# A new issue order, new engines for the evacuations and new PSUM places in a one-core kernel of a long convolution and a token-mixing MLP

## The chip, the core and the metric

The kernel runs on one core of a Trainium2 chip. A core has five engines with a queue of instructions each: PE (TensorE, matmuls; PEld are its weight loads), DVE (VectorE), ACT (ScalarE), POOL (GpSimd) and SP (SyncE, which here only issues transfers). Each queue runs in order, and queues wait for one another by semaphores. Transfers issued from SP, from POOL and, once, from ACT are carried out by DMA engines, 16 for the core. The metric is the device time of one execution in microseconds: the median of three runs before the change is 170.21 (170.05 to 170.65). A profile shows one execution, with times counted from its first instruction.

## The reference, cut to what matters

```python
def _A_ref(q, k, v, shift_k, ssm_k, ssm_D):      # S = 2048 positions, D = 448 channels
    k_shift = sum of 4 shifted copies of k, each times a column of shift_k
    kv = k_shift * v
    y = irfft(rfft(kv, 2S) * rfft(ssm_k, 2S))[:S]          # a causal convolution over S
    y = y.astype(bfloat16) + kv * ssm_D
    return q * y

def _B_ref(x, w1, b1, w2, b2):                   # S = 2048, F = 1792
    h = _layernorm(x, axis=-1)
    u = _gelu(jnp.einsum("bsd,sf->bdf", h, w1) + b1)
    y = jnp.einsum("bdf,fs->bds", u, w2) + b2
    return y transposed to (b, s, d)

x = A_q
h = x + _A_ref(_layernorm(x), A_k, A_v, A_shift_k, A_ssm_k, A_ssm_D)
return h + _B_ref(_layernorm(h), B_w1, B_b1, B_w2, B_b2)
```

## The kernel before

A position s is 16 q + r: partition q (128 of them) and row r (16 rows of 448 channels). The convolution is made of matmuls with tables of sines: two transform stages forward, a product, two stages back. Every operation belongs to a step with a name, a number, and a place in the step: k1.9:8 is the operation 8 of step 9 of the group k1. The groups, in the order of the data:

- **dummy**: matmuls on a constant at the very start. **tables**: the tables of sines (made by VectorE from iotas of POOL, then a Sin on ScalarE: tables.5:3 and tables.6:3 give the two halves of E, tables.7:5 the small table FW and its relations), and the identity ID (tables.3:0). tables.0:5 is a Sin of one element.
- **loads**: on SP. loads.0 to 3 are the four parts of ssm_k (0.5, 0.5, 0.5 and 0.25 MB); loads.4 is shift_k; 5, 6, 8 and 10 are k's row groups 3, 0, 1 and 2; 7, 9, 11 and 12 are v's 0, 1, 2 and 3 (0.46 MB each); 13 and 14 are D and the biases. **xload**: four row groups of x; groups 2 and 3 share memory with two of four shuffle buffers and wait for the last u shuffle.
- **kv**: kv.1 to kv.8 transpose k (two steps for each row group, in the order 3, 0, 1, 2) and copy it out; kv.9 to kv.16 are the shifted product, two steps for each row group: matmuls with the diagonals DG (kv.0:4), then a multiplication by v on VectorE (L1006). **kT**: ssm_k transposed, eight steps.
- **k1, u1** (`emit_stage1`): first transform stage of the kernel ssm_k and of kv. 16 steps each: eight matmuls of 32 columns (L1058), one evacuation of 896 elements (operation 8), and after every second step three shuffles, two on POOL (9, 10) and one on SP (11), at L1074. Four steps share one of four shuffle buffers; a buffer is free when its shuffles have landed.
- **k2, u2** (`emit_stage2`): second stage; four matmuls a step (L1093, 64 columns), evacuations 4 and 5 in the odd step.
- **i1** (`emit_products_i1`): 16 products on VectorE (L1160, step operation 0; the first waits for every shuffle), matmuls (L1177), evacuations, and shuffles into TZ (L1201; L1188 for the last step, i1.16).
- **q, xn**: statistics of the 16 rows of x on VectorE (L1237) and their roots on POOL; xn normalises rows 0 to 3 (L1270 on ScalarE, L1272 on VectorE). **ct, ct0**: transposed tables. **warm**, **ew**, **bias**: small things.
- **i2** (`emit_i2`): the last stage and the layernorm of h, row by row: matmuls (L1303, L1309), a gate (L1319 or L1321), a combine on VectorE (L1329, L1339), squares on ScalarE (L1357), a chain on POOL, and Q[r] on VectorE (L1388). i2.8 makes Q[0], i2.21 combines row 3; i2.58, i2.67 up to i2.97 are matmuls of rows 9 to 15, and rows 14 and 15 (i2.93, i2.97) need the small transfers of TZ's last columns.
- **w1a, w1b, w2**: loads of the MLP's weights on SP: four parts of W1A (0.917 MB, four rows r each; the last three wait for the last TZ shuffles), four of W1B, four of W2.
- **mlp** (`emit_mlp`): mlp.0 to 15: row r times seven column blocks of W1A, in seven PSUM banks (L1435); mlp.17 to 23: the other seven blocks, 16 matmuls each (L1445), Gelu on ScalarE (L1425); mlp.24 to 39: output row r, 14 matmuls (L1457), an evacuation with the residual on VectorE (L1460), output transfers. mlp.39, the last row, is cut in a part of 320 (0 to 13) and one of 128 columns (16 to 29).

Nothing chooses at run time. `ORDER` lists, for each of the five queues, the operations in the order in which they are issued; where an operation may run on two engines (an evacuation, xn, a gate), the list in which it stands decides. `SLOTS` gives every group of matmuls its PSUM bank or pair of banks, and every shuffle or product buffer its place, in the order of use. `schedule` walks these lists with estimated times only to find which operation is the last to be waited for; `emit` writes out instructions and semaphore waits. The rest of the file says what each operation computes.

## Time and profile before

| | us |
|---|---|
| median of three runs | 170.21 |
| span of the profiled execution | 168.7 |
| PE busy | 160.0 |
| DVE busy | 101.7 |
| ACT busy | 90.3 |
| POOL busy | 58.8 |

The profiled execution's own span is 168.7 us from its first instruction to its last; 1.5 us lie around it in the timed median. A view by windows gives, for each stretch, its length, the busy time of PE, PEld, DVE, ACT and POOL with the number of instructions, the granted clock of PE (1.00 is full), the busy share of the DMA engines and GB/s. The chain of waits lists the work that ended last, back to what released it, as start, length and what. A timeline merges instructions of one kind that follow each other; in brackets stands how long the engine was idle before, and who released it. A line of the view of one source line gives the least, median and greatest duration in ns and the first and last start.

### The profile page before, as it was taken

To read this page: it belongs to the slowest core of one execution; us is meant where nothing else is said; L and a number is where in the kernel's file an instruction comes from. 1 tells how busy PE (TensorE), PEld (TensorE's weight loads), DVE (VectorE), ACT (ScalarE), POOL (GpSimd) and SP (SyncE) were. 2 spreads that over 40 slices of the span, in tenths; PEclk is the share of its full clock that TensorE was granted. 3 is DMA by queue.
4 is the path that set the end of the run, shared out by engine and by line. 5 is a ranking of instruction groups with operands and counts; after the bars stand their busy time and mean duration, and the time that the engine had idled before them with its cause. 6 is when DMAs were issued, how large, how long until landed. Compare 5 with 4: busy or idle time off the path is not lost.

```text
span 168.7 us, 3563 instructions
## 1 busy us (share of the span) xinstructions
PE 160.0 (95%) x1416; PEld 92.4 (55%) x1416; DVE 101.7 (60%) x191; ACT 90.3 (54%) x130; POOL 58.8 (35%) x155
## 2 busy tenths in 40 slices
...
## 3 DMA queue, kind: packets, MB, share of 16 engines
q1 hardware_dynamic: 12396, 28.26, 46.1%
...
## 4 chain that ended last, share of the span: by engine, by line
PE 62%; ACT 15%; DVE 10%; DMA 6%; issue 3%; POOL 1%; DVEq 0%; ACTq 0%; POOLq 0%
PE ps L1457 25%; PE ps L1435 13%; PE ps L1445 13%; ACT arena L738 7%; DMA arena<-arena 6%; ACT arena L1068 4%; ACT arena L739 4%; DVE arena L1160 2%; PE ps L1309 2%; PE ps L1058 2%; PE ps L1037 2%; PE ps L1093 2%; DVE arena L741 2%; DVE arena L837 1%; PE ps L1177 1%
## 5 line engine op out<-in xcount | busy, mean ns | idle before, releaser
L1460 DVE SCALAR_TENSOR_TENSOR arena<-ps,arena 128x448 bf16<-128x448 f32 (+2 forms) x17 | 11.1, 656 | 55.8 <-PE ps L1457 55.8
L1457 PE MATMUL ps<-arena 128*128 128x448 bf16 (+2 forms) x238 | 42.7, 342 | 0.0
L1457 PEld LDWEIGHTS ps<-arena 128*128 128x128 bf16 x238 | 33.3, 145 | 9.5
L1435 PE MATMUL ps<-arena 128*128 128x448 bf16 x112 | 23.5, 353 | 0.0
L738 ACT CAST arena<-ps 128x896 bf16<-128x896 f32 (+1 forms) x29 | 23.1, 933 | 0.0
L1068 ACT CAST arena<-ps 128x896 bf16<-128x896 f32 x24 | 20.2, 920 | 4.8 <-PE ps L1058 3.3
L1445 PE MATMUL ps<-arena 128*128 128x448 bf16 x112 | 22.3, 352 | 0.0
L1074 POOL DMA_DIRECT2D arena<-arena x32 | 17.7, 558 | 8.6 <-ACT arena L1068 8.5
L1425 ACT ACTIVATE arena<-ps,arena 128x448 bf16<-128x448 f32 x14 | 8.2, 632 | 19.3 <-PE ps L1445 10.3
L1093 PE MATMUL ps<-arena 128*64 128x448 bf16 x128 | 15.3, 361 | 2.0 <-ACT arena L739 0.9
L1435 PEld LDWEIGHTS ps<-arena 128*128 128x128 bf16 x112 | 10.7, 98 | 10.8 <-DVE arena L1388 1.3
L1445 PEld LDWEIGHTS ps<-arena 128*128 128x128 bf16 x112 | 11.0, 98 | 10.2
L1160 DVE TENSOR_TENSOR arena<-arena 128x1792 bf16<-128x1792 bf16 x16 | 16.5, 1084 | 0.0
L1177 PE MATMUL ps<-arena 64*128 64x448 bf16 x128 | 14.1, 351 | 1.1 <-ACT arena L738 0.5
L1058 PE MATMUL ps<-arena 128*32 128x448 bf16 x256 | 14.6, 355 | 0.5 <-ACT arena L1068 0.2
L1201 POOL DMA_DIRECT2D arena<-arena x16 | 9.3, 586 | 13.8 <-ACT arena L738 12.9
L1093 PEld LDWEIGHTS ps<-arena 128*64 128x64 f16 x128 | 5.3, 108 | 11.2 <-ACT arena L739 3.4
L1177 PEld LDWEIGHTS ps<-arena 64*128 64x128 f16 x128 | 5.2, 94 | 9.8 <-DVE arena L1160 3.1
L1388 DVE TENSOR_SCALAR arena<-arena 128x448 bf16<-128x448 f32 x16 | 7.6, 509 | 4.8 <-POOL arena L1381 4.8
L1058 PEld LDWEIGHTS ps<-arena 128*32 128x32 f16 x256 | 5.1, 95 | 7.8 <-ACT arena L1068 2.6
L1237 DVE BATCH_NORM_STATS2 arena<-arena 128x6 f32<-128x448 bf16 x16 | 9.4, 612 | 0.0
L739 ACT ACTIVATE arena<-ps 128x896 bf16<-128x896 f32 x10 | 8.6, 926 | 0.8 <-PE ps L1093 0.8
...
## 6 DMA issues: line engine op xcount, KB each, us to landing
...
```

Source lines behind the costliest of these rows:

```text
L738: return e.copy(out=dst(), in_=src())
L739: return e.activation(out=dst(), in_=src(), func=ACT.Copy, scale=scale)
L1058: op("pe", lambda e, W, b=b, r=r, q=q, x=x, c0=c0: e.matmul(PS[32 * q:32 * q + 32, b.slots[x], 0:D], E[:, 2 * r + x, c0:c0 + 32], src[:, r ...
L1068: return e.copy(out=dst, in_=Ppair(b)) if W == "act" else e.tensor_copy(out=dst, in_=Ppair(b))
L1074: shuf[tag].append(op(q_, lambda e, W, g=g, i=i, a=a, nu=nu, jh=jh: e.dma_start(T[a + i:a + i + 4 * nu - 3:4].rearrange("p (j k) c d -> p ...
L1093: op("pe", lambda e, W, b=bs[h], h=h, j=j, c=c, par=par: e.matmul(PS[64 * par:64 * par + 64, b.slots[c], 0:D], FW[:, 64 * c:64 * c + 64], ...
L1160: op("dve", lambda e, W, m=m, i=i: e.tensor_tensor(out=MR(m.slots[0]).rearrange("p (x y) d -> p x y d", x=2), in0=TU[:, i].unsqueeze(2).br ...
L1177: k = op("pe", lambda e, W, b=bs[h], m=ms[h], par=par, t=t, tab=tab, xy=xy, P=P: e.matmul(Pb(b, par), tab[P, :], MR(m.slots[0])[P, xy, :], ...
L1435: op("pe", lambda e, W, r=r, fc=fc, b=bs[fc]: e.matmul(Pb(b), W1A[:, r, 128 * fc:128 * fc + 128], Q[:, r, :], start=(r == 0), stop=(r == R ...
L1445: op("pe", lambda e, W, r=r, fc=fc, b=b: e.matmul(Pb(b), W1B[:, r, 128 * (fc - n0):128 * (fc - n0) + 128], Q[:, r, :], start=(r == 0), sto ...
L1457: op("pe", lambda e, W, r=r, fc=fc, b=b, d0=d0, d1=d1: e.matmul(Pb(b)[:, d0:d1], W2[fc // 7][:, fc % 7, r:S:R], G[:, fc, d0:d1], start=(fc ...
L1460: op("dve", lambda e, W, r=r, b=b, A=A, d0=d0, d1=d1: e.scalar_tensor_tensor(out=XR(r)[:, d0:d1], in0=Pb(b)[:, d0:d1], scalar=bm[:, r:r + ...
```

## The change

Both lists are replaced as a whole; no operation is added or taken away, and the functions stay as they are. The new lists come from a search of order, engines and places whose model of the transfers lets all queues share the 16 DMA engines. All lines behind the lists move down by 24.

31 operations change between ScalarE and VectorE. To VectorE go kv.6:12, ct0.0:8, bias.0:1, ten evacuations of 896 elements (u1.1, u1.2, u1.8, u1.11, u1.13, k2.5:5, k2.9:5, k2.15:4, u2.11:4, u2.3:5) and the gate i2.68. To ScalarE go kT.1 to kT.5 (without kT.0), kv.7:8, seven evacuations of 896 elements (k1.12, u1.3, u1.12, u1.15, k2.9:4, i1.10:18, i1.6:9), xn.1 and the gates i2.55, i2.81, i2.85. The diff, cut:

```diff
--- before.py
+++ after.py
     "pe": (
-        "dummy.0:1-9 kv.4:0-11 kv.3:0-7 kv.6:0-11 kv.5:0-7 kT.1:0-7 kT.0:0-3 kT.1:9-11 kT.0:4-7 kT.3:0-7 "
-        "kT.2:0-3 kT.3:9-11 kT.5:0-7 kT.2:4-7 ct0.0:0-7 kT.6:0-7 kT.7:0-7 bias.0:0 kv.7:0-7 k1.8:0-7 k1.9:0-7 "
-        "k1.12:0-7 k1.10:0-7 kv.1:0-7 kv.2:0-11 k1.11:0-7 k1.15:0-7 k1.14:0-7 k1.13:0-7 kT.4:0-7 kv.8:0-11 "
...
-        "i2.54:0-1 i2.28:0-1 i2.32:0-1 warm.1:0 mlp.0:2-6 i2.58:0-1 mlp.0:0-1 mlp.1:0-6 i2.67:0-1 mlp.2:0-6 "
...
-        "mlp.36:0-13 mlp.37:0-13 mlp.38:0-13 mlp.39:0-10 mlp.39:16-17 mlp.39:11 mlp.39:18-20 mlp.39:12 "
-        "mlp.39:21-22 mlp.39:13 mlp.39:23-29 "
+        "dummy.0:1-9 kv.3:0-7 kv.4:0-11 kv.1:0-7 kv.2:0-11 kv.7:0-7 kv.8:0-11 kT.4:0-7 kv.9:0-27 kv.10:0-23 kT.5:0-7 "
+        "kT.1:0-7 kT.1:9-11 u1.0:0-7 u1.1:0-7 kT.6:0-7 kT.7:0-7 u1.2:0-7 u1.3:0-7 kT.3:0-7 kv.5:0-7 kT.3:9-11 "
+        "kT.0:0-7 kT.2:0-7 k1.8:0-7 k1.12:0-7 kv.15:0-27 k1.9:0-7 kv.6:0-11 k1.10:0-7 k1.0:0-7 k1.11:0-7 k1.13:0-7 "
+        "kv.12:0-23 k1.14:0-7 k1.1:0-7 k1.15:0-7 k1.2:0-7 kv.14:0-23 k1.4:0-7 k1.5:0-7 kv.11:0-27 k1.6:0-7 k1.7:0-7 "
+        "k1.3:0-7 u1.4:0-7 kv.13:0-27 u1.5:0-7 u1.6:0-7 kv.16:0-23 u1.7:0-7 u1.8:0-7 u1.9:0-7 u1.10:0-7 u1.11:0-7 "
+        "ct0.0:0-7 u1.12:0-7 u1.13:0-7 u1.14:0-7 u1.15:0-7 k2.12:0-3 k2.13:0-3 k2.0:0-3 k2.1:0-3 k2.6:0-3 k2.7:0-3 "
+        "k2.9:0-3 k2.8:0-3 k2.10:0-3 k2.11:0-3 k2.4:0-3 k2.5:0-3 k2.14:0-3 k2.15:0-3 u2.0:0-3 u2.1:0-3 u2.8:0-3 "
+        "u2.9:0-3 u2.12:0-3 u2.13:0-3 u2.4:0-3 u2.5:0-3 u2.7:0-3 u2.6:0-3 i1.1:10-17 i1.1:1-8 k2.3:0-3 k2.2:0-3 "
...
+        "ct.0:0-7 ct.1:0-7 bias.0:0 i2.1:0-3 i2.9:0-3 ct.2:0-7 i2.10:0-1 i2.2:0-1 warm.0:0 i2.45:0-1 i2.28:0-1 "
+        "i2.17:0-1 i2.54:0-1 i2.41:0-1 warm.1:0 i2.20:0-1 i2.58:0-1 i2.32:0-1 mlp.0:2 mlp.0:1 mlp.0:3 mlp.0:0 "
+        "i2.67:0-1 mlp.1:1 mlp.0:5 mlp.1:3 mlp.1:0 mlp.1:2 mlp.0:6 i2.71:0-1 mlp.0:4 mlp.1:5-6 mlp.2:0 mlp.2:5 "
+        "mlp.2:1-2 mlp.1:4 i2.80:0-1 mlp.2:3 mlp.2:6 mlp.3:1 mlp.3:6 mlp.2:4 mlp.3:5 i2.84:0-1 mlp.3:2 mlp.3:4 "
+        "mlp.3:0 mlp.3:3 mlp.4:4 mlp.4:6 i2.93:0-1 mlp.4:1 mlp.5:6 mlp.5:4 mlp.4:2-3 mlp.4:5 mlp.5:1 mlp.5:5 mlp.4:0 "
+        "mlp.6:6 mlp.6:1 mlp.5:2 i2.97:0-1 mlp.5:0 mlp.6:5 mlp.5:3 mlp.6:3 mlp.7:5 mlp.7:3 mlp.6:0 mlp.7:0 mlp.8:0 "
+        "mlp.6:4 mlp.8:3 mlp.9:0 mlp.10:0 mlp.7:1 mlp.8:1 mlp.9:1 mlp.9:3 mlp.6:2 mlp.19:0 mlp.7:4 mlp.8:5 mlp.10:1 "
+        "mlp.19:1 mlp.10:3 mlp.7:6 mlp.8:4 mlp.7:2 mlp.19:2 mlp.9:4 mlp.10:4 mlp.19:3 mlp.8:2 mlp.11:3-4 mlp.11:1 "
...
+        "mlp.38:9 mlp.35:13 mlp.39:5-6 mlp.38:10 mlp.39:7-9 mlp.36:12-13 mlp.38:11-12 mlp.39:24 mlp.38:13 mlp.39:25 "
+        "mlp.39:10 mlp.39:26-29 mlp.39:11-13 "
     ),
     "act": (
     "act": (
-        "tables.0:5 kv.4:12 kv.3:8 kv.6:12 tables.5:3 tables.6:3 ct0.0:8 bias.0:1 tables.7:5 k1.8:8 k1.9:8 "
-        "k1.10:8 k1.11:8 k1.13:8 k1.14:8 k1.15:8 k1.4:8 u1.0:8 u1.1:8 u1.2:8 u1.4:8 k1.5:8 k1.6:8 k1.7:8 u1.5:8 "
-        "u1.6:8 u1.7:8 u1.8:8 u1.9:8 k2.1:4 k2.13:5 k2.5:4-5 k2.9:5 u1.10:8 u1.13:8 u1.14:8 u1.11:8 k2.3:4 "
-        "k2.7:4 k2.11:4 k2.15:4-5 u2.13:4 u2.1:4 u2.9:4-5 u2.7:4-5 i1.1:9 i1.1:18 u2.11:4 i1.14:9 i1.14:18 "
-        "u2.11:5 i1.8:9 i1.8:18 i1.10:9 u2.5:4-5 u2.3:5 i1.12:9 i1.12:18 u2.3:4 i1.6:18 u2.15:5 u2.15:4 i1.4:17 "
...
+        "tables.5:3 kv.3:8 kv.4:12 kT.4:8 kv.7:8 kT.5:8 kT.1:8 u1.0:8 tables.6:3 kT.3:8 u1.3:8 kT.2:8 k1.12:8 k1.8:8 "
+        "k1.9:8 k1.10:8 k1.11:8 k1.13:8 k1.14:8 k1.15:8 tables.0:5 k1.4:8 k1.5:8 k1.6:8 k1.7:8 u1.4:8 u1.5:8 u1.6:8 "
+        "u1.7:8 u1.9:8 u1.10:8 tables.7:5 u1.12:8 u1.14:8 u1.15:8 k2.13:5 k2.1:4 k2.7:4 k2.9:4 k2.11:4 k2.5:4 "
+        "k2.15:5 u2.1:4 u2.9:4-5 u2.13:4 u2.5:4-5 u2.7:4 i1.1:18 u2.7:5 i1.1:9 k2.3:4 i1.14:18 i1.14:9 i1.10:18 "
+        "u2.11:5 i1.10:9 i1.8:9 i1.8:18 i1.6:18 u2.3:4 i1.6:9 i1.12:18 i1.12:9 u2.15:4-5 i1.4:8 i1.4:17 xn.1:0 "
+        "i1.16:9 i1.16:18 xn.2:0 ct.0:8 xn.5:0 ct.2:8 ct.1:8 xn.4:0 i2.46:0 i2.29:0 i2.55:0 i2.19:0 i2.59:0 i2.22:0 "
...
     ),
     "dve": (
-        "dummy.0:0 tables.3:0-1 kv.0:3 tables.6:0 tables.4:16 tables.5:0 tables.4:17 tables.6:1 tables.4:18 "
-        "tables.5:1 tables.4:19 tables.6:2 tables.4:20 tables.5:2 kT.1:8 tables.7:6 kT.0:8 kT.3:8 tables.7:4 "
-        "tables.7:7 kv.5:8 kT.5:8 kT.2:8 kT.7:8 kT.6:8 bias.1:0 kv.7:8 k1.12:8 kv.1:8 kv.2:12 kv.0:4 kT.4:8 "
-        "kv.8:12 kv.12:25 kv.12:24 kv.9:28 kv.10:24 kv.9:29 kv.10:25 kv.11:28-29 k1.0:8 k1.1:8 u1.3:8 q.1:2 "
-        "kv.13:28-29 q.2:0 kv.14:25 kv.14:24 k1.2:8 k1.3:8 q.2:2 q.1:0 kv.15:29 kv.15:28 k2.1:5 q.2:1 q.2:3 "
-        "k2.13:4 q.4:0 q.1:1 kv.16:25 kv.16:24 k2.9:4 q.1:3 u1.12:8 u1.15:8 q.3:2 k2.3:5 k2.7:5 k2.11:5 q.4:2 "
-        "q.3:3 u2.13:5 q.3:0 u2.1:5 i1.0:0 i1.1:0 i1.13:0 i1.14:0 i1.9:0 i1.7:0 i1.8:0 i1.10:0 i1.12:0 i1.11:0 "
-        "i1.10:18 q.4:3 xn.0:1 i1.5:0 i1.6:0 i1.3:0 i1.6:9 xn.3:1 i1.2:0 i1.16:0 q.4:1 q.3:1 i1.15:0 q.6:0 q.6:2 "
-        "q.5:0 q.5:2 q.6:3 q.5:3 q.5:1 q.8:2 q.6:1 q.8:3 q.7:2 q.8:0 xn.1:0 i2.3:0 i2.11:0 i2.4:0 i2.12:0 i2.5:0 "
-        "i2.13:0 i2.6:0 i2.18:0 i2.21:0 i2.8:0 i2.14:0 i2.55:0 i2.30:0 i2.16:0 q.7:0 i2.34:0 i2.26:0 q.8:1 q.7:1 "
-        "q.7:3 i2.27:0 i2.47:0 i2.43:0 q.8:4 i2.56:0 i2.39:0 i2.40:0 i2.60:0 i2.81:0 i2.69:0 i2.52:0 i2.73:0 "
...
+        "dummy.0:0 tables.5:0-1 tables.3:0 tables.5:2 tables.6:0 kv.0:3 kv.1:8 kv.2:12 kv.0:4 kv.8:12 tables.6:1 "
+        "tables.3:1 kv.9:29 kv.9:28 kv.10:24-25 tables.6:2 u1.1:8 kT.6:8 u1.2:8 kv.5:8 kT.7:8 q.1:2 kT.0:8 q.2:0 "
+        "q.2:2 q.1:3 kv.15:28-29 kv.6:12 q.2:1 k1.0:8 q.4:0 kv.12:25 kv.12:24 q.2:3 k1.1:8 k1.2:8 kv.14:25 "
+        "tables.4:16 kv.14:24 tables.4:17 kv.11:28-29 tables.4:18 q.1:0 tables.4:19 k1.3:8 q.4:1 tables.4:20 q.1:1 "
+        "kv.13:29 tables.7:7 tables.7:6 kv.13:28 kv.16:24-25 u1.8:8 tables.7:4 u1.11:8 ct0.0:8 u1.13:8 q.4:2 k2.13:4 "
+        "k2.1:5 k2.7:5 k2.9:5 k2.11:5 k2.5:5 k2.15:4 u2.1:5 i1.0:0 u2.13:5 i1.1:0 i1.14:0 i1.10:0 i1.9:0 i1.13:0 "
+        "k2.3:5 i1.5:0 i1.7:0 i1.8:0 i1.6:0 u2.11:4 i1.12:0 i1.11:0 u2.3:5 i1.2:0 i1.3:0 q.3:0 xn.0:1 i1.15:0 q.4:3 "
+        "i1.16:0 q.6:0 q.3:1 q.6:2 q.3:2 xn.3:1 q.6:3 q.6:1 q.5:0 q.3:3 q.8:0 q.5:2 q.5:1 q.5:3 q.8:2 q.7:2 q.7:0 "
+        "i2.11:0 i2.3:0 i2.12:0 i2.4:0 bias.0:1 i2.5:0 q.8:1 i2.6:0 i2.18:0 q.7:3 i2.13:0 q.7:1 i2.14:0 i2.8:0 "
+        "i2.21:0 i2.16:0 q.8:3 i2.30:0 i2.68:0 i2.34:0 i2.26:0 q.8:4 i2.43:0 i2.60:0 i2.27:0 i2.47:0 i2.56:0 i2.39:0 "
+        "i2.69:0 i2.40:0 i2.73:0 i2.86:0 i2.52:0 i2.82:0 i2.66:0 i2.53:0 i2.65:0 i2.95:0 i2.78:0 i2.79:0 i2.99:0 "
+        "bias.1:0 i2.92:0 i2.91:0 i2.105:0 i2.104:0 mlp.25:14 mlp.26:14 mlp.29:14 mlp.28:14 mlp.27:14 mlp.24:14 "
+        "mlp.30:14 mlp.33:14 mlp.31:14 mlp.34:14 mlp.32:14 mlp.37:14 mlp.35:14 mlp.36:14 mlp.38:14 mlp.39:30 "
+        "mlp.39:14 "
     ),
     "pool": (
-        "tables.4:0 tables.4:2 tables.4:4 tables.4:6 tables.4:8 tables.4:10 tables.4:12 tables.4:14 tables.4:1 "
-        "tables.4:3 tables.4:5 tables.4:7 tables.4:9 tables.4:11 tables.4:13 tables.4:15 tables.1:0 tables.0:1 "
-        "tables.0:2 tables.0:0 tables.0:3 tables.0:4 loads.13:0 tables.2:0 tables.2:1 tables.2:3 tables.2:5 "
-        "tables.2:7 tables.2:8 tables.2:9 tables.2:10 tables.2:11 tables.2:2 tables.2:4 tables.2:6 q.0:0 q.0:1 "
-        "kv.0:1 kv.0:2 tables.7:0 tables.7:1 tables.7:2 tables.7:3 tables.7:8 tables.7:9 tables.7:10 tables.7:11 "
-        "kv.0:0 k1.9:9 k1.9:10 k1.11:9 k1.11:10 k1.13:9 k1.13:10 k1.15:9 k1.15:10 u1.1:9 u1.1:10 k1.1:9 k1.1:10 "
-        "u1.3:9 u1.3:10 k1.5:9 k1.5:10 u1.5:9 u1.5:10 k1.7:9 k1.7:10 u1.7:9 u1.7:10 u1.9:9 u1.9:10 k1.3:9 "
-        "k1.3:10 q.2:4 q.2:5 q.1:4 xn.3:0 q.1:5 u1.13:9 u1.13:10 u1.11:9 u1.15:9 u1.15:10 u1.11:10 xn.0:0 ew.0:0 "
-        "ew.0:2 ew.0:3 ew.0:1 i1.1:19 i1.1:21 i1.14:19 i1.14:21 i1.8:21 i1.8:19 i1.10:19 i1.10:21 i1.12:19 "
...
+        "tables.1:0 tables.0:2 tables.0:0 tables.0:4 tables.0:3 tables.0:1 tables.2:10 tables.2:7 tables.4:1 "
+        "tables.4:5 tables.2:9 loads.13:0 kv.0:1 tables.2:3 kv.0:2 tables.2:6 q.0:0 tables.2:8 kv.0:0 u1.1:9 u1.3:10 "
+        "u1.3:9 tables.2:5 tables.4:4 tables.4:9 tables.4:8 tables.2:11 k1.9:10 u1.1:10 tables.4:14 tables.4:13 "
+        "tables.4:10 tables.4:7 k1.11:10 k1.9:9 tables.4:15 tables.2:2 tables.4:2 k1.11:9 k1.13:9 tables.4:6 "
+        "tables.4:0 tables.2:0 tables.4:11-12 q.2:4 tables.4:3 k1.13:10 k1.1:9 tables.2:4 k1.1:10 k1.15:10 k1.15:9 "
+        "k1.5:9 tables.2:1 k1.5:10 k1.7:9 tables.7:1 k1.7:10 k1.3:10 tables.7:2 tables.7:0 tables.7:3 k1.3:9 u1.7:10 "
+        "u1.9:10 tables.7:8 u1.9:9 u1.5:10 u1.13:9 tables.7:9 q.0:1 u1.13:10 tables.7:10 u1.5:9 u1.15:9 u1.7:9 "
+        "u1.11:9-10 u1.15:10 tables.7:11 q.2:5 q.1:4-5 ew.0:0 ew.0:2 ew.0:1 i1.1:19 i1.1:21 i1.14:19 i1.14:21 "
+        "i1.10:19 i1.10:21 i1.8:19 i1.8:21 ew.0:3 xn.0:0 i1.6:19 i1.6:21 i1.12:21 i1.12:19 i1.4:20 xn.3:0 i1.4:19 "
...
     ),
     "sp": (
-        "loads.6:0 loads.8:0 loads.0:0 loads.1:0 loads.2:0 loads.3:0 loads.13:1 loads.14:0 loads.14:1 loads.10:0 "
-        "loads.5:0 loads.11:0 loads.4:0 loads.4:1 loads.4:2 loads.12:0 loads.9:0 loads.7:0 k1.9:11 k1.11:11 "
-        "k1.13:11 k1.15:11 xload.0:0 xload.1:0 u1.1:11 k1.1:11 u1.3:11 k1.5:11 u1.5:11 k1.7:11 u1.7:11 u1.9:11 "
-        "k1.3:11 u1.13:11 u1.11:11 u1.15:11 ct0.1:0 ct0.1:1 xload.2:0 xload.3:0 w1a.0:0 ct0.1:2 ct0.1:4 ct0.1:3 "
-        "ct0.1:5 i1.1:20 i1.1:22 i1.14:20 i1.14:22 i1.8:20 i1.8:22 i1.10:20 i1.10:22 i1.12:20 i1.12:22 i1.6:22 "
-        "i1.4:18 i1.16:19 i1.16:20 w1a.1:0 w1a.2:0 w1a.3:0 w1b.0:0 w1b.0:1 w1b.0:2 w1b.0:3 w2.0:0 w2.0:1 w2.0:2 "
-        "w2.0:3 mlp.25:15 mlp.27:15 mlp.29:15 mlp.31:15 mlp.33:15 mlp.35:15 mlp.37:15 mlp.38:15 mlp.39:31 "
+        "loads.6:0 loads.5:0 loads.4:2 loads.10:0 loads.4:1 loads.4:0 loads.2:0 loads.7:0 loads.0:0 loads.3:0 "
+        "loads.1:0 loads.14:0 loads.8:0 xload.0:0 loads.14:1 xload.1:0 loads.12:0 loads.13:1 loads.9:0 loads.11:0 "
+        "u1.1:11 u1.3:11 k1.11:11 k1.9:11 k1.15:11 k1.13:11 k1.7:11 k1.5:11 k1.1:11 k1.3:11 u1.7:11 u1.9:11 u1.5:11 "
+        "u1.13:11 u1.15:11 u1.11:11 ct0.1:1 ct0.1:0 xload.3:0 xload.2:0 w1a.0:0 ct0.1:4 ct0.1:3 ct0.1:5 ct0.1:2 "
+        "i1.14:22 i1.10:22 i1.4:18 i1.16:20 i1.16:19 w1a.1:0 i1.1:20 i1.12:22 i1.14:20 i1.1:22 i1.12:20 i1.8:20 "
+        "i1.6:22 i1.10:20 i1.8:22 w1a.2:0 w1a.3:0 w1b.0:0-3 w2.0:0-3 mlp.29:15 mlp.25:15 mlp.27:15 mlp.33:15 "
+        "mlp.31:15 mlp.35:15 mlp.37:15 mlp.38:15 mlp.39:31 "
     ),
 }
...
```

102 rows, old and new, of tables (ORDER, SLOTS) are left out of this document.

## Prediction

> **What bounds the kernel now.** I read the page first, then the windows, the chain of waits, the timelines of ScalarE and VectorE, and last the landing times of the transfers.
>
> ```profile
> span 168.7 us, 3563 instructions
> PE 160.0 (95%) x1416; PEld 92.4 (55%) x1416; DVE 101.7 (60%) x191; ACT 90.3 (54%) x130; POOL 58.8 (35%) x155
> ```
> ```profile
> 5.00:10.00 5.00, 4.90 (x72) 3.99 (x70) 4.99 (x11) 4.26 (x4) 2.49 (x4) 1.00 1.05 377
> 5.74:70.94 65.20, 61.15 (x876) 30.81 (x874) 62.58 (x95) 59.57 (x71) 35.59 (x67) 1.00 0.80 267
> 2.23:69.01 66.78, 62.99 (x879) 31.57 (x877) 64.16 (x98) 57.89 (x69) 36.64 (x83) 1.00 0.81 274
> 78.26:166.20 87.94, 87.92 (x476) 56.16 (x476) 27.22 (x63) 22.10 (x48) 14.25 (x38) 1.00 0.44 171
> 80.00:84.00 4.00, 4.00 (x23) 2.08 (x23) 4.00 (x16) 2.65 (x7) 3.15 (x7) 1.00 1.06 390
> ```
> ```profile
> 1.52 0.57 POOL arena L779 x2
> ...
> 2.25 1.21 DVE arena L837
> ...
> 4.74 0.60 DVE arena L841
> ...
> 6.09 1.14 DVE arena L844
> ...
> 21.55 6.04 DMA arena<-arena
> ...
> 69.06 0.95 PE ps L1177 x8
> ...
> 70.03 0.91 ACT arena L738
> ...
> 78.26 1.10 PE ps L1435 x5
> ...
> 94.38 1.51 PE ps L1445 x8
> ...
> 123.70 42.08 PE ps L1457 x231
> ...
> 165.81 0.55 DVE arena L1460
> ```
>
> Two machines stand one behind the other. From 78.26 to 166.20 PE is busy 87.92 of 87.94 us at full clock: 476 matmuls, 1.51/8 = 0.19 us for a wide one. No order makes that shorter; it can start earlier or be interrupted. Before it, PE's busy share says little, because there it waits for evacuations: ScalarE is busy 59.57 of the 65.20 us from 5.74 to 70.94, VectorE 64.16 of the 66.78 us from 2.23 to 69.01. The chain passes from the last product to the i1 matmuls (69.06) and the last i1 evacuation (70.03), and i1 ends at 70.94. So the front is bound by ScalarE and VectorE together, with 5.6 and 2.6 us of waiting left in it.
>
> ```profile
> 5.74 2.84 ACT L738 COPY arena<-ps 128x1024 bf16<-128x1024 bf16 x3 [3.23 <-PE ps L965]
> 8.47 3.91 ACT L847 ACTIVATE arena<-arena 128x2048 f16<-128x2048 int32 x2
> ...
> 23.05 0.91 ACT L1068 CAST arena<-ps 128x896 bf16<-128x896 f32 x1 [2.33 <-PE ps L1058]
> ...
> 27.66 5.76 ACT L1068 CAST arena<-ps 128x896 bf16<-128x896 f32 x7 [1.02 <-PE ps L991]
> ...
> 47.98 22.96 ACT L738 CAST arena<-ps 128x896 bf16<-128x896 f32 x28
> ...
> 71.74 2.07 ACT L1270 ACTIVATE arena<-arena 128x448 f32<-128x448 bf16 x3
> ```
> ```profile
> 11.06 1.88 DVE L741 COPY arena<-ps 128x1024 bf16<-128x1024 bf16 x3
> ...
> 20.19 4.38 DVE L1006 TENSOR_TENSOR arena<-ps,arena 128x256 bf16<-128x256 f32 x8
> ...
> 43.58 3.10 DVE L742 TENSOR_SCALAR arena<-ps 128x896 bf16<-128x896 f32 x3
> ...
> 50.05 10.22 DVE L1160 TENSOR_TENSOR arena<-arena 128x1792 bf16<-128x1792 bf16 x10
> ...
> 67.95 1.06 DVE L1160 TENSOR_TENSOR arena<-arena 128x1792 bf16<-128x1792 bf16 x1
> ...
> 68.92 2.19 DVE L1237 BATCH_NORM_STATS2 arena<-arena 128x6 f32<-128x448 bf16 x4
> ...
> 73.95 1.28 DVE L1339 SCALAR_TENSOR_TENSOR arena<-ps,arena 128x448 f32<-128x448 f32 x2 [0.37 <-PE ps L1309]
> ```
>
> The reader sees two prices per evacuation: 896 elements cost ScalarE 22.96/28 = 0.82 us and VectorE 3.10/3 = 1.03; 1024 bf16 elements cost (8.47 - 5.74)/3 = 0.91 from start to start and 1.88/3 = 0.63. He also sees ScalarE's two large holes. At 23.05 it waits 2.33 us, because the last v load lands late and eight kv products then follow in one block on VectorE (4.38 us from 20.19), their matmuls ahead of k1's on PE. At 27.66 it waits 1.02 us, after a shuffle that took 6.04 us to land beside the two x loads.
>
> **The change, part by part.** The arithmetic is the same, so the sum is made of moves. I take the profiled span, 168.7; the median of the runs, 170.21, lies 1.5 above it, and that distance is added back.
>
> (a) Evacuations change engines. ScalarE gives up ten of 896 elements, kv.6 and ct0.0 (12 moves with bias.0, a trifle): 10 x 0.82 + 2 x 0.91 = 10.0 us. It gets seven of 896 elements, five kT, kv.7 and xn.1 (2.07/3 = 0.69): 7 x 0.82 + 6 x 0.91 + 0.69 = 11.9. With bias.0 that is 1.8 us more before i1's end. VectorE gets 10 x 1.03 + 2 x 0.63 = 11.6 and gives 7 x 1.03 + 6 x 0.63 = 11.0, and one bn_stats (2.19/4 = 0.55) moves behind i1: 0.0 to -0.3. So the change adds about 1.5 us of work to a front that both engines bound. It must win it back in waits.
>
> (b) ScalarE begins with tables.5's Sin instead of three copies that wait for k. VectorE now makes tables.5 first, right after POOL's iota (1.52 and 0.57): 1.21 + 0.60 + 1.14, with ID (0.3) between, end near 5.2, where the first copy began at 5.74. Worth -0.5 (bounds -0.8, 0).
>
> (c) Loads. k3 and k2 move to places 2 and 4 of SP's queue, v0 to 8, x0 and x1 ahead of v3, v1, v2. Up to v0 lie 2.36 MB; at the 377 GB/s of 5 to 10 us, begun near 2.5, they are in by 9 to 10 us, and kv.9 and kv.10 run at 10.5 to 12.5. The other six kv pairs are then spread one by one between k1 evacuations, and no x load runs beside the k1 shuffles. So the block at 20.19 and the 6.04 us landing lose their causes: -2.33 and -1.02. New waits: I followed the queues by hand from 19 to 38 us. k1.4 waits for u1.0's buffer (u1.1's shuffle is issued on POOL behind k1.9's, near 22, and lands by the row below at 25.8): 0.6; k1.6 waits for kv.11's matmuls: 0.3; u1.5 for kv.13's: 0.35. That makes 1.25. Bounds: none of it, or all of the 3.35 back.
>
> ScalarE: 70.94 + 1.8 - 0.5 - 3.35 + 1.25 = 70.1, so i1 ends **0.8 earlier**. VectorE as a check: by the same hand count its 2.6 us of waits become 1.2 for k3, k2 and kv.5 in its first 17 us and 0.6 later on, so its last product ends at 69.01 - 0.15 - 2.6 + 1.8 = 68.1, 0.9 earlier. Two engines, one answer; I keep -0.8. Ends: -2.0 with no new wait, +1.3 with all old ones back.
>
> (d) From the last product to the first MLP matmul. VectorE has nine bn_stats behind its last product instead of seven (+1.1), not xn.1 (0.5 less), Q of row 0 now stands ahead of the combine of row 3 (0.6 less), and the wait of 0.37 at 73.95 becomes work: +0.15. i2.58 moves ahead of mlp.0, into time in which PE waits for that Q: 2 x 0.19 = -0.38.
>
> (e) The MLP on PE: same matmuls, chains now shuffled together. W2, at the rate of 390 GB/s behind W1, lands 7 us or more ahead of each first use, though that comes 12 us earlier for its first chunk. What gets tight is SP: after w1a.1 nine small TZ transfers now stand ahead of w1a.2.
>
> ```profile
> L1074 POOL DMA_DIRECT2D arena<-arena x32: 547/547/811, 16.3 to 45.7; - x32
> ...
> DMA to landing us min/median/max: 2.4/3.9/6.0
> ```
> ```profile
> L1201 SPq DMA_DIRECT2D arena<-arena x12: 666/666/683, 54.6 to 69.2; - x12
> ...
> DMA to landing us min/median/max: 3.1/3.7/4.2
> ```
> ```profile
> 75.20 1.47 SPq L1408 DMA_DIRECT2D arena<-in_B_w_dram  x3
> 76.72 7.27 SPq L1412 DMA_DIRECT2D arena<-in_B_w_dram  x4
> ```
>
> Nine issues of 0.666 make 6.0 us. Count from the landing of i1's last transfers (75.20 before, 3.1 us ahead of mlp.0; 3.4 after). w1a.2 is issued 6.5 us later instead of 0.5; three chunks of 0.917 MB at 390 GB/s take 7.05, start and landing 2.3 to 3.0 (estimated from the first w1a issue and the rate), so w1b.0 lands at 16 to 16.6. Its first use, mlp.19:0, is the 73rd matmul after mlp.0 starts: 13.6 + 3.4 = 17.0. Slack 0.4 to 1.0, where before it was several us. i2.93 needs the last small transfer: 0.5 + 8 x 0.666 + 3.1 to 4.2 = 8.9 to 10.0, need 7.2 + 3.4 = 10.6. The rows Q[8] to Q[15] are also wanted 1.5 to 4 us earlier than before, and VectorE's queue there has, by count, under 1 us to spare. I take +0.1; bounds 0 and 2.35, one chunk.
>
> (f) The tail. The last PE work is now the 320-wide part of row 15, and its evacuation comes last. Before, that evacuation (0.55) ran beside seven narrow matmuls, with 0.3 for the narrow one behind it. +0.15, and +0.1 for rows that end bunched and their output transfers: +0.25 (0 to 0.6).
>
> Sum: -0.8 + 0.15 - 0.38 + 0.1 + 0.25 = **-0.7**: span 168.0, median 169.5.
>
> [...] The row says 3.9 in the median. [...]
>
> **The rivals.** (1) *Late u shuffles; slower.* POOL's queue holds u1.7:9, u1.11:9, u1.11:10 and u1.15:10 behind u1.15:9, which waits for the very last u1 evacuation, near 38. At 0.55 each, with the table products between them, the last issue starts near 42.2 by my count, and i1.0, the first product, waits for every shuffle. By the median it lands at 46.1, just behind the time when VectorE comes to i1.0 (45.8, eight k2 and u2 evacuations of 1.03 after 37.6); by the 6.0 of the row at 48.2. Every us behind 46 is a us of i1's end, and the gain is gone from 46.8 on. For: in the profile above the shuffles often took four us and more, and POOL now makes its tables in between. Against: no load runs at that time. At 6.0: +2.1 - 0.3, median 171.3.
>
> (2) *W1 late; slower.* The slack of (e) is missed by a chunk: PE stands at mlp.19:0 or i2.93 for 2.3 us. For: slack under one us. Against: the rate of 390 held steadily. 169.5 + 2.3 - 0.7 of slack: 171.1.
>
> (3) *No change.* The new waits are as long as the old ones less the work added: the model that placed the transfers is no nearer to the chip, and the new order does not do what it says. i1's end moves by 0, the rest by +0.1: 170.3.
>
> (4) *More.* (c) leaves no new wait: -1.25 more, and (b) its full 0.8: 168.0.
>
> **How the numbers follow.** A difference under 0.3%, 0.5 us, cannot be told from none. Forecast 0.42, of which 0.28 lies below 169.7; rival (4) 0.14; (3) 0.10, of which 0.03 slower; (1) 0.17; (2) 0.17. Faster 0.28 + 0.14 = 0.42; same 0.14 + 0.07 = 0.21; slower 0.03 + 0.34 = 0.37. The forecast's own range, from the ends of (b) and (c), is 168.3 to 170.6; with the rivals the range is 167.7 to 171.9.
>
> **What would show it.** (a) ScalarE with 59 instead of 62 evacuations of 896 elements ahead of i1's end, busier by 1.8 us up to there. (b) Sin first on ScalarE, near 5.2. (c) No hole over 1 us on ScalarE between 15 and 38; kv.9's products before 12.5; the shuffle at k1.4 landing by 26. i1's end near 70.1, mlp.0 near 77.2. (e) PE without a gap over 0.3 us at mlp.19:0 and i2.93; nine L1201-type issues on SP behind w1a.1. (f) The last VectorE instruction is the 320-wide one. I am wrong if VectorE or ScalarE stands idle for over 1 us ahead of i1.0 (rival 1), if PE is idle between 84 and 95 (rival 2), or if i1 ends no earlier than 70.9.

## Result: 3.7% slower, and the profile after

| | median, us | lowest to highest | profiled execution's span |
|---|---|---|---|
| before | 170.43 | 170.05 to 171.15 | 168.7 |
| after | 176.94 | 176.02 to 178.24 | 174.2 |

The ratio is 1.0373, with the interval [1.0319, 1.0427]: the new lists make the kernel **slower by 6.5 us** in the median. The forecast was 169.5 with a range of 167.7 to 171.9, so both were wrong. The profiled execution after the change took 176.02, the lowest of the four; its span is 5.5 us longer than that of before, and those 5.5 us are looked for below. The last microsecond of the 6.5 is therefore not placed by the profile. All ratios below are worked out from each kernel's undisturbed executions alone; the profiles of the first kernel of "Repairs together" (175.71 us) and of "old PE rows and banks" (184.03) are of slower ones, and that of the third (174.30) is of the slowest one counted.

The page of the kernel after, first its span and engines:

```profile
span 174.2 us, 3568 instructions
PE 160.5 (92%) x1416; PEld 92.3 (53%) x1416; DVE 100.3 (58%) x188; ACT 93.4 (54%) x133; POOL 61.4 (35%) x155
```

PE's busy time is nearly the same (160.5 against 160.0), with the same 1416 matmuls. The view by windows (start and end, length, busy time of PE, PEld, DVE, ACT and POOL, granted clock, DMA share, GB/s) over ScalarE's and VectorE's stretch up to i1's end, from there to the first MLP matmul, and over two parts of the MLP:

```profile
5.09:72.82 67.73, 61.96 (x896) 32.55 (x893) 63.32 (x100) 61.75 (x73) 35.88 (x86) 1.00 0.79 258
2.23:70.35 68.12, 62.40 (x878) 32.40 (x876) 63.68 (x95) 59.28 (x70) 36.28 (x92) 1.00 0.80 264
72.82:80.88 8.06, 6.37 (x37) 2.97 (x37) 7.61 (x23) 7.43 (x13) 6.03 (x10) 1.00 0.58 178
80.88:101.00 20.12, 18.00 (x91) 8.16 (x90) 14.98 (x45) 14.44 (x35) 16.22 (x37) 1.00 0.88 322
101.00:171.46 70.46, 70.46 (x386) 46.94 (x383) 10.15 (x17) 8.54 (x14) 0.00 (x0) 1.00 0.29 118
```

Four terms come out of these stretches and the rows that bound them. i1 ends at 72.82 instead of 70.94: **+1.88**. From there to the first MLP matmul pass 8.06 us instead of 78.26 - 70.94 = 7.32: **+0.74**. From that matmul to PE's end pass 171.46 - 80.88 = 90.58 instead of 87.94: **+2.64**; PE is busy 18.00 of the first 20.12 us and all of the 70.46 after them, so the loss lies ahead of 101. The tail is 174.2 - 171.46 = 2.74 instead of 168.7 - 166.20 = 2.50: **+0.24**. Together +5.5. The granted clock is 1.00 throughout, so no part of this is a lower clock.

The timeline of ScalarE after, around the new waits of the front (start, length, what; in brackets the idle time before it and who ended it):

```profile
5.09 2.00 ACT L871 ACTIVATE arena<-arena 128x2048 f16<-128x2048 int32 x1 [3.09 <-DVE arena L868]
...
9.60 1.93 ACT L762 COPY arena<-ps 128x1024 bf16<-128x1024 bf16 x2 [0.69 <-PE ps L1061]
11.91 1.01 ACT L762 COPY arena<-ps 128x1024 bf16<-128x1024 bf16 x1 [0.39 <-PE ps L1061]
13.51 1.01 ACT L762 COPY arena<-ps 128x1024 bf16<-128x1024 bf16 x1 [0.59 <-PE ps L1061]
...
28.78 6.81 ACT L1092 CAST arena<-ps 128x896 bf16<-128x896 f32 x8 [1.18 <-PE ps L1082]
...
43.55 1.73 ACT L763 ACTIVATE arena<-ps 128x896 bf16<-128x896 f32 x2 [0.83 <-PE ps L1117]
...
70.81 2.01 ACT L762 CAST arena<-ps 128x896 bf16<-128x896 f32 x2
```

The old holes of the kernel before (2.33 at 23.05, 1.02 at 27.66) are gone. In their place stand many small ones: three at the kT copies (0.69, 0.39, 0.59), 1.18 at k1.4, 0.83 at the second stage. Who made ScalarE wait is read one step further back, on PE:

```profile
8.85 0.71 PE L1061 MATMUL ps<-arena 128*128 128x128 bf16 x8 [0.32 <-DMA arena<-in_A_ssm_k_dram]
...
12.76 0.72 PE L1061 MATMUL ps<-arena 128*128 128x128 bf16 x8 [0.88 <-DMA arena<-in_A_ssm_k_dram]
...
37.13 0.62 PE L1131 MATMUL ps<-arena 128*128 128x128 f16 x8 [0.87 <-DVE arena L1092]
...
42.59 1.71 PE L1117 MATMUL ps<-arena 128*64 128x448 bf16 x16 [0.89 <-DVE arena L766]
...
91.67 0.74 PE L1459 MATMUL ps<-arena 128*128 128x448 bf16 x3 [0.52 <-DVE arena L1412]
...
93.79 1.69 PE L1459 MATMUL ps<-arena 128*128 128x448 bf16 x8 [0.24 <-DVE arena L1412]
...
96.50 1.31 PE L1459 MATMUL ps<-arena 128*128 128x448 bf16 x6 [1.02 <-DVE arena L1412]
```

At 8.85 and 12.76 the transposes of ssm_k wait for its load, 1.20 us together. The line L1412 at 91.67 to 96.50 is VectorE's Q: the MLP's first matmuls wait for rows of the layernorm. VectorE itself had waited, and the timelines of VectorE and POOL say for whom:

```profile
91.10 0.51 DVE L1412 TENSOR_SCALAR arena<-arena 128x448 bf16<-128x448 f32 x1 [0.76 <-POOL arena L1405]
...
95.93 0.93 DVE L1412 TENSOR_SCALAR arena<-arena 128x448 bf16<-128x448 f32 x2 [1.17 <-POOL arena L1405]
```
```profile
29.83 2.17 POOL L1098 DMA_DIRECT2D arena<-arena  x4
...
36.85 1.68 POOL L1098 DMA_DIRECT2D arena<-arena  x3
...
90.35 0.72 POOL L1405 TENSOR_TENSOR arena<-arena 128x2 f32<-128x2 f32 x1
```

How full PE itself was while the front ran, up to 36 us, show the windows of the two kernels, before and then after:

```profile
4.71:36.00 31.29, 30.05 (x564) 19.57 (x565) 29.31 (x51) 25.13 (x29) 17.35 (x33) 1.00 0.95 336
4.71:36.00 31.29, 29.83 (x583) 19.78 (x581) 27.81 (x55) 26.80 (x30) 14.17 (x45) 1.00 0.89 302
```

PE was busy 30.05 of 31.29 us there before, ScalarE only 25.13. L1405 is the last link of POOL's chain for the layernorm, an operation on 128x2 elements, and here it takes 0.72 us. The two rows of L1098 are shuffle issues of the first stage; they come up again where the order of the shuffles is tried.

### The profile page after: what moved, and what is told of

Read it like the earlier page. It is cut to its first block, busy times and chain, and to the rows that moved or that the text cites. A ratio compares the mean times of both kernels' runs of the same rounds, so it can differ in the third digit from the quotient of the medians.

```text
span 174.2 us, 3568 instructions
## 1 busy us (share of the span) xinstructions
PE 160.5 (92%) x1416; PEld 92.3 (53%) x1416; DVE 100.3 (58%) x188; ACT 93.4 (54%) x133; POOL 61.4 (35%) x155
## 4 chain that ended last, share of the span: by engine, by line
PE 59%; DMA 12%; ACT 12%; POOL 7%; issue 3%; SPq 3%; DVE 3%; ACTq 0%; POOLq 0%
PE ps L1481 24%; PE ps L1469 12%; DMA arena<-arena 8%; PE ps L1459 6%; ACT arena L762 6%; PE ps L1201 5%; DMA arena<-in_A_ssm_k_dram 4%; PE ps L1117 4%; ACT arena L1092 3%; PE ps L1082 2%; PE ps L1061 2%; POOL arena L1405 2%; ACT arena L763 2%; DVE arena L1484 1%; POOL arena L1394 1%
## 5 line engine op out<-in xcount | busy, mean ns | idle before, releaser
L1481 PE MATMUL ps<-arena 128*128 128x448 bf16 (+2 forms) x238 | 46.6, 342 | 0.0
L1484 DVE SCALAR_TENSOR_TENSOR arena<-ps,arena 128x448 bf16<-128x448 f32 (+2 forms) x17 | 10.5, 653 | 60.3 <-PE ps L1481 60.1
L1481 PEld LDWEIGHTS ps<-arena 128*128 128x128 bf16 x238 | 32.9, 144 | 11.1 <-DVE arena L1484 0.5
L1469 PE MATMUL ps<-arena 128*128 128x448 bf16 x112 | 27.7, 352 | 0.0
L1459 PE MATMUL ps<-arena 128*128 128x448 bf16 x112 | 25.9, 353 | 1.9 <-DVE arena L1412 1.8
L762 ACT CAST arena<-ps 128x896 bf16<-128x896 f32 x28 | 23.5, 1071 | 0.2 <-PE ps L1117 0.2
L1098 POOL DMA_DIRECT2D arena<-arena x32 | 17.9, 565 | 14.4 <-PE ps L1061 12.2
L1092 ACT CAST arena<-ps 128x896 bf16<-128x896 f32 x23 | 19.4, 918 | 2.4 <-PE ps L1082 1.8
L1459 PEld LDWEIGHTS ps<-arena 128*128 128x128 bf16 x112 | 10.5, 98 | 13.3 <-DVE arena L1412 4.3
L1469 PEld LDWEIGHTS ps<-arena 128*128 128x128 bf16 x112 | 11.0, 98 | 9.2 <-ACT arena L1449 0.2
L762 ACT COPY arena<-ps 128x1024 bf16<-128x1024 bf16 (+1 forms) x11 | 11.3, 1074 | 2.0 <-PE ps L1061 2.0
L1412 DVE TENSOR_SCALAR arena<-arena 128x448 bf16<-128x448 f32 x16 | 7.8, 511 | 5.0 <-POOL arena L1405 4.9
L1381 ACT ACTIVATE arena<-arena 128x448 bf16<-128x448 f32 x14 | 8.0, 571 | 3.8 <-DVE arena L1353 3.7
L1333 PE MATMUL ps<-arena 128*128 128x448 bf16 x32 | 7.8, 353 | 1.9 <-DMA arena<-arena 1.6
```

The source lines that it names most:

```text
L762: return e.copy(out=dst(), in_=src())
L1092: return e.copy(out=dst, in_=Ppair(b)) if W == "act" else e.tensor_copy(out=dst, in_=Ppair(b))
L1098: shuf[tag].append(op(q_, lambda e, W, g=g, i=i, a=a, nu=nu, jh=jh: e.dma_start(T[a + i:a + i + 4 * nu - 3:4].rearrange("p (j k) c d -> p ...
L1459: op("pe", lambda e, W, r=r, fc=fc, b=bs[fc]: e.matmul(Pb(b), W1A[:, r, 128 * fc:128 * fc + 128], Q[:, r, :], start=(r == 0), stop=(r == R ...
L1469: op("pe", lambda e, W, r=r, fc=fc, b=b: e.matmul(Pb(b), W1B[:, r, 128 * (fc - n0):128 * (fc - n0) + 128], Q[:, r, :], start=(r == 0), sto ...
L1481: op("pe", lambda e, W, r=r, fc=fc, b=b, d0=d0, d1=d1: e.matmul(Pb(b)[:, d0:d1], W2[fc // 7][:, fc % 7, r:S:R], G[:, fc, d0:d1], start=(fc ...
```

## The experiments

The theory after this reading: the MLP loses because its matmuls, shuffled across rows, ask for Q sooner than POOL's chain makes it; the front loses because the ssm_k loads land late and because POOL's shuffles are not issued in the order in which they are ready. The rivals: the MLP's loss is that of the weights behind the nine small transfers on SP; and, for the front, that ScalarE and VectorE are bound by their work, so that any wait taken away comes back elsewhere. All kernels start from one of the two kernels' lists and leave every operation as it is, so all compute the same thing. "Front" is all up to the end of i1; "i2 order" is the order from there to the first MLP matmul. Stage times are read from the one profiled execution of each, and "MLP on PE" runs from the first MLP matmul to PE's end. The kernels after, new front alone, old PE rows and banks and rows in order have the same lists up to i1's end, yet their profiles end it at 72.82, 73.32, 73.14 and 72.33: a difference of under a microsecond between two single profiles says little.

| kernel | median, us | ratio to before | i1 end | first MLP matmul | MLP on PE |
|---|---|---|---|---|---|
| before | 170.43 | | 70.94 | 78.26 | 87.94 |
| after | 176.94 | 1.0373 [1.0319, 1.0427] | 72.82 | 80.88 | 90.58 |
| new front alone | 174.06 | 1.0190 [1.0156, 1.0224] | 73.32 | 81.17 | 88.69 |
| new rest alone | 176.69 | 1.0358 [1.0318, 1.0398] | 70.91 | 79.22 | 92.75 |
| one shuffle earlier | 176.81 | 1.0352 [1.0307, 1.0397] | 72.09 | 80.38 | 90.61 |
| ssm_k ahead of v0 | 178.89 | 1.0479 [1.0424, 1.0534] | 74.40 | 82.89 | 90.61 |
| tables early | 178.41 | 1.0442 [1.0402, 1.0481] | 72.82 | 81.14 | 90.58 |
| old PE rows and banks | 182.43 | 1.0664 [1.0609, 1.0719] | 73.14 | 84.12 | 95.63 |
| new front, TZ early | 173.86 | 1.0185 [1.0159, 1.0212] | 73.48 | 81.85 | 88.05 |
| rows in order | 175.72 | 1.0292 [1.0258, 1.0326] | 72.33 | 80.78 | 89.35 |
| shuffles when ready | 175.44 | 1.0274 [1.0253, 1.0295] | 71.52 | 79.90 | 90.59 |
| both repairs | 172.23 | 1.0108 [1.0072, 1.0145] | 71.79 | 79.61 | 88.05 |

### Which half costs what: the new front alone, the new rest alone

The first kernel takes the new lists up to i1 and, on SP, to the end but for the output transfers, with the old order, engines and banks of ct, i2 and the MLP; the second does the opposite.

```diff
 "pe", new front alone
-mlp.0:2 mlp.0:1 mlp.0:3 mlp.0:0 i2.67:0-1 mlp.1:1 mlp.0:5 mlp.1:3
+mlp.0:2-6 i2.58:0-1 mlp.0:0-1 mlp.1:0-6 i2.67:0-1 mlp.2:0-6
...
 "pe", new rest alone
-mlp.0:2-6 i2.58:0-1 mlp.0:0-1 mlp.1:0-6 i2.67:0-1 mlp.2:0-6
+mlp.0:2 mlp.0:1 mlp.0:3 mlp.0:0 i2.67:0-1 mlp.1:1 mlp.0:5 mlp.1:3
```

> The new lists up to i1, SP's list too (without the order of the output transfers), with the order, engines and banks of before for ct, i2 and the MLP. Theory A (the loss is made in separate places: 1.9 us up to i1's end, 0.7 from there to mlp.0, 2.6 in the MLP where rows of Q are asked for before they are made, 0.3 in the tail): only the 1.9 of the front and up to 0.5 behind it remain, 172.3 to 172.8, and PE has no wait for Q over 0.3 us in the MLP. Rival B (the MLP's waits are the late front carried on, whose statistics and Q begin 2 us later): PE still waits 2 us for Q, 174 to 175. Rival C (W1 late, since nine small transfers stand ahead of w1a.2): PE waits over 1 us for a transfer at mlp.19:0 or i2.93, 174.

> The opposite mixture: the lists of before up to i1 with SP's list of before, and the new order, engines and banks for ct, i2 and the MLP. Theory A: 170.4 + 2.6 + 0.3 and up to 0.7 behind i1 = 173.3 to 174.0, and PE waits about 2 us for Q between mlp.4 and mlp.12. Rival B: i1 ends as before and Q is in time, 170.4 to 171.0. Rival C: W1 is issued 6 us earlier here, so nothing is late, 170.4 to 171.0.

With the new front alone the time is 174.06, not the 172.3 to 172.8 that the theory gave but the time that stood for its rivals: i1 ends late (73.32), later than in the kernel after with the same lists, and the MLP is nearly whole (88.69 us). Its PE and window rows:

```profile
98.64 0.93 PE L1439 MATMUL ps<-arena 128*128 128x448 bf16 x4 [0.45 <-DMA arena<-in_B_w_dram]
```
```profile
81.17:101.00 19.83, 19.32 (x101) 9.40 (x101) 14.16 (x40) 13.95 (x34) 13.71 (x37) 1.00 0.86 296
```

In the old order PE does not wait for Q; in the same stretch it does 101 matmuls where the kernel after does 91. The one wait of size is that for W1 at 98.64, 0.45 us: the place that the second rival named, at a fifth of its price.

The second kernel, 176.69 where the theory gave 173.3 to 174.0, is a poor complement. With the old front a root on POOL came late, a gate on ScalarE stood 3.63 us for it, and PE behind the gate. ScalarE, then PE, then the windows of that kernel:

```profile
87.94 0.72 ACT L1337 ACTIVATE arena<-ps,arena 128x448 f32<-128x448 f32 x1 [3.63 <-POOL arena L1266]
```
```profile
88.72 0.93 PE L1327 MATMUL ps<-arena 128*128 128x448 bf16 x2 [3.10 <-ACT arena L1337]
89.44 2.42 PE L1453 MATMUL ps<-arena 128*128 128x448 bf16 x6
92.08 2.43 PE L1453 MATMUL ps<-arena 128*128 128x448 bf16 x12
```
```profile
85.00:90.00 5.00, 1.90 (x8) 0.68 (x6) 3.05 (x10) 1.59 (x4) 3.49 (x8) 0.83 1.05 401
90.00:95.00 5.00, 5.00 (x24) 2.37 (x22) 3.42 (x9) 4.84 (x14) 3.74 (x10) 0.83 1.05 412
```

Its MLP of 92.75 us therefore holds a stall and a slow clock that the kernel after does not have, and the two ratios do not add up to that of the whole change (1.9% and 3.6% against 3.7%). What it does give is the stretch between: with i1's end at 70.91 as before, the first MLP matmul comes at 79.22 instead of 78.26, with the last TZ transfers landing 4.28 us behind i1's end (4.26 before). So the new order of the rest costs up to a microsecond there by itself, as far as one profile of each can say.

### The MLP: rows, banks, weights

"Rows in order" keeps the banks, places and everything else of the kernel after and only sorts the chains of rows 0 to 15 by row, leaving the i2 matmuls and mlp.19 in their places. The chains of mlp.17 and on move behind row 15. "Old PE rows and banks" keeps everything up to mlp.0, and i2 on all engines, in the order after the change; the matmuls of the MLP, the banks from i2.67 on, the MLP's Gelus, evacuations and output transfers take the old order, row by row.

```diff
 "pe", rows in order
-mlp.0:2 mlp.0:1 mlp.0:3 mlp.0:0 i2.67:0-1 mlp.1:1 mlp.0:5 mlp.1:3 mlp.1:0 mlp.1:2 mlp.0:6 i2.71:0-1 mlp.0:4
+mlp.0:2 mlp.0:1 mlp.0:3 mlp.0:0 i2.67:0-1 mlp.0:5 mlp.0:6 mlp.0:4 mlp.1:2 mlp.1:1 mlp.1:3 i2.71:0-1 mlp.1:0
...
```

> The changed kernel with its banks and the places of its i2 matmuls kept, the matmuls of mlp.0 to mlp.15 alone sorted row by row (the chains of mlp.17 and on move behind them, but for mlp.19). By count Q[6] is then asked for 10.3 us after mlp.0, Q[7] at 11.8, Q[10] at 16, and they are made 10.7, 12.9 and 15.5 us after it in the changed kernel. Theory A: one wait of 1.1 to 1.4 us at mlp.7 is left of the 2.9 us of waits, 175.2 to 176.0. If the waits have another cause than the order in which rows are asked for: 2.5 to 3 us of waits stay, 176.6 to 177.2.

> The changed kernel with the MLP's matmuls alone (their banks, Gelus, evacuations and output transfers too) in the order of before, row by row; i2 on the other engines, the front and SP's loads stay as changed. Theory A (the new order asks for rows of Q before POOL and VectorE have made them): the three waits for Q at mlp.6:6, mlp.7:5 and mlp.10:0 (0.69 + 0.41 + 1.18) go, 2.0 to 2.6 gained: 174.3 to 174.9. Rival C (what is late are W1 and the last TZ columns behind nine small transfers on SP): PE waits for transfers instead, and at most 1.0 is gained, 175.9 or more.

Sorting the rows brought 1.2 us (175.72 against 176.94), within what the theory gave, and the MLP on PE became 90.58 - 89.35 = 1.23 us shorter. The waits for Q fell from 1.8 us to one of 0.31 in its timeline; beside it PE now waits 0.29 and 0.25 us for gates on ScalarE that hold its banks:

```profile
82.56 0.36 PE L1456 MATMUL ps<-arena 128*128 128x448 bf16 x1 [0.29 <-ACT arena L1340]
83.18 0.93 PE L1456 MATMUL ps<-arena 128*128 128x448 bf16 x4 [0.25 <-ACT arena L1340]
...
93.97 2.25 PE L1456 MATMUL ps<-arena 128*128 128x448 bf16 x11 [0.31 <-DVE arena L1409]
```

So the interleaving of rows is about half of the term, and banks and i2 order are bound up with the other half. The second kernel, 182.43 where the theory had 174.3 to 174.9, is inconclusive: the old banks under the new order of the gates made mlp.0:2 wait 2.23 us for a gate that shares its bank, and all later rows stood behind it, the first 14 matmuls at 4.51/14 = 0.32 us in the mean, where 0.19 is usual. PE, and the window around it:

```profile
84.11 4.51 PE L1430 MATMUL ps<-arena 128*128 128x448 bf16 x14 [2.23 <-ACT arena L1314]
```
```profile
84.00:88.00 4.00, 3.89 (x12) 1.70 (x13) 0.00 (x0) 0.61 (x3) 0.39 (x1) 0.57 0.50 122
```

"TZ early" tests the second rival. It is the new front alone, with the nine small TZ transfers put ahead of w1a.1 on SP again:

```diff
 "sp", new front, TZ early
-i1.14:22 i1.10:22 i1.4:18 i1.16:20 i1.16:19 w1a.1:0 i1.1:20 i1.12:22 i1.14:20 i1.1:22 i1.12:20 i1.8:20
-i1.6:22 i1.10:20 i1.8:22 w1a.2:0
+i1.1:20 i1.1:22 i1.14:20 i1.14:22 i1.10:20 i1.10:22 i1.8:20 i1.8:22 i1.6:22 i1.12:22 i1.12:20 i1.4:18
+i1.16:20 i1.16:19 w1a.1:0 w1a.2:0
```

> The mixture of the new front with the old MLP once more (174.06), with SP's nine small TZ transfers issued as their evacuations come, ahead of w1a.1, as before the change. If W1 was late there (waits of 0.22 at mlp.4:4 and 0.61 at mlp.19:4): they go, 173.1 to 173.5. If they have another cause: 173.8 to 174.3.

The wait for W1 is gone and the MLP takes 88.05 us, as before (87.94). But the transfers that now stand in front land 5.32 us behind i1's end instead of 4.87, the first MLP matmul comes 8.37 us behind it instead of 7.85, and the median is the same: 173.86 against 174.06. The rival's mechanism is real, and moving the transfers was worth nothing either way.

### The front: one shuffle, one load, the tables

Three single moves in the new kernel. The first issues u1.1's second POOL shuffle ahead of five table operations and of one of k1.9's, since k1.4 waits for its buffer; the second loads the first ssm_k part ahead of v0; the third makes all tables before the first shuffle, so that none stands between shuffles on POOL (with the VectorE and ScalarE operations that follow from them).

```diff
 "pool", one shuffle earlier
-u1.1:9 u1.3:10 u1.3:9 tables.2:5 tables.4:4 tables.4:9 tables.4:8 tables.2:11 k1.9:10 u1.1:10
+u1.1:9 u1.3:10 u1.3:9 u1.1:10 tables.2:5 tables.4:4 tables.4:9 tables.4:8 tables.2:11 k1.9:10
...
 "sp", ssm_k ahead of v0
-loads.2:0 loads.7:0 loads.0:0
+loads.2:0 loads.0:0 loads.7:0
...
 "pool", tables early
-tables.2:8 kv.0:0 u1.1:9 u1.3:10
+tables.2:8 kv.0:0 tables.4:0 tables.4:2-4 tables.4:6-15 tables.2:0-2 tables.2:4-5 tables.2:11 tables.7:1-2
+tables.7:0 tables.7:3 tables.7:8-11 u1.1:9 u1.3:10
```

> The changed kernel with one operation moved: u1.1:10 on POOL stands right behind u1.3:9 instead of behind k1.9:10, which waits for ScalarE. Theory A: u1.1's shuffle is issued 2.2 us earlier, the wait of 1.18 us ahead of k1.4 falls under 0.3, and i1 ends up to 0.9 earlier: 176.0 to 176.4. Rival D (the front is held by ScalarE's and VectorE's work and by the PSUM banks of k2, so a wait that goes here comes back behind it): k1.4's wait falls, but i1's end does not move by more than 0.3, 176.6 to 177.2.

> The changed kernel with one load moved: loads.0, a quarter of ssm_k, ahead of v's first row group on SP. Theory A: PE's wait of 0.88 us at kT.1 (12.76) falls under 0.3 and ScalarE's copies behind it start 0.5 to 0.9 earlier, i1 ends up to 0.9 earlier, 176.0 to 176.6. Rival D: kv.9's products wait for v as long, or the wait comes back behind; 176.6 to 177.2.

> The changed kernel with the small tables made early: POOL's iotas, memsets and tables.7 operations stand in its 12 us of idle time ahead of u1.1:9 instead of between the shuffles, with the VectorE and ScalarE steps of tables.4 and tables.7 moved ahead accordingly. Theory E (POOL's tables hold up the shuffles: k1.3:9 is issued at 36.9 and lands near 42, which is the wait of 0.89 us at k2.6, and the last u shuffle is issued at 45.3): k1.3:9 is issued near 34.5, the wait at k2.6 falls under 0.3, the last u shuffle is issued by 43.5, i1 ends 0.8 to 1.5 earlier: 175.4 to 176.1. Rival F (the DMA engines are full from 36 to 44, their share 0.97 to 1.02, so earlier issues land as late): the issues are earlier, the landings are not, and i1's end moves by 0.3 at most: 176.6 to 177.2.

None of them gained, where the theory gave them 0.3 to 1.5 us each. ScalarE with the one shuffle earlier:

```profile
27.70 1.71 ACT L1090 CAST arena<-ps 128x896 bf16<-128x896 f32 x2 [0.62 <-PE ps L1080]
...
42.80 1.73 ACT L761 ACTIVATE arena<-ps 128x896 bf16<-128x896 f32 x2 [1.01 <-PE ps L1115]
```

The wait at k1.4 fell from 1.18 to 0.62 where under 0.3 was expected, and a small part came back at the second stage, which waits 1.01 instead of 0.83. The profile ends i1 0.73 earlier, but ScalarE's waits among the kT copies, ahead of the shuffle that was moved, are 0.69 less in it, so most of this is not the shuffle's doing. The median of 176.81 is unchanged. With ssm_k ahead of v0, VectorE's kv products and then PE:

```profile
13.94 2.22 DVE L1028 TENSOR_TENSOR arena<-ps,arena 128x512 bf16<-128x512 f32 x4 [3.51 <-DMA arena<-in_A_v_dram]
```
```profile
9.76 0.71 PE L1059 MATMUL ps<-arena 128*128 128x128 bf16 x8 [1.40 <-DMA arena<-in_A_ssm_k_dram]
16.21 0.94 PE L1080 MATMUL ps<-arena 128*32 128x448 bf16 x16 [2.12 <-DVE arena L1028]
```

The products now start at 13.94, after 3.51 us of waiting for v (10.60 in the kernel after), and the kernel is 2 us slower. So moving v0 back costs more than it saves, and the waits for ssm_k are the price of having v0 early. With the tables early the kernel is 1.5 us slower in the median (178.41); its profile, of an execution of 176.27 us, ends i1 at 72.82 as after the change and does not show why. PE's waits at k1's tail are no better in it (three waits of PE in that kernel):

```profile
37.67 0.62 PE L1127 MATMUL ps<-arena 128*128 128x128 f16 x8 [0.95 <-DVE arena L1088]
40.46 1.73 PE L1113 MATMUL ps<-arena 128*64 128x448 bf16 x16 [0.54 <-ACT arena L1088]
42.56 1.70 PE L1113 MATMUL ps<-arena 128*64 128x448 bf16 x16 [0.37 <-DVE arena L762]
```

### The front: shuffles in order of readiness

What two of the three had in common is POOL's queue. In the kernel after, k1.15's second POOL shuffle is the third of the four issues at 29.83, long behind its evacuation, and holds the buffer that u1.8 needs; k1.3's comes at 36.85 behind three table products; u1.5's and u1.7's stand behind later ones. This kernel has the tables early and, besides, all shuffles of k1 and u1 on POOL and SP in the order in which their evacuations end:

```diff
 "pool", shuffles when ready (tables ahead of the first)
-u1.1:9 u1.3:10 u1.3:9
...
-k1.1:9 k1.1:10 k1.15:10 k1.15:9 k1.5:9
...
-k1.3:9 u1.7:10 u1.9:10 u1.9:9 u1.5:10 u1.13:9 u1.13:10 u1.5:9 u1.15:9 u1.7:9 u1.11:9-10 u1.15:10
+u1.1:9-10 u1.3:9-10 k1.9:9-10 k1.11:9-10 k1.13:9-10 k1.15:9-10 k1.1:9-10 k1.5:9-10 k1.7:9-10 k1.3:9-10
+u1.5:9-10 u1.7:9-10 u1.9:9-10 u1.11:9-10 u1.13:9-10 u1.15:9-10
```

> The changed kernel with the tables early as before, and the shuffles of k1 and u1 on POOL and SP in the order in which their evacuations end (u1.1 u1.3 k1.9 k1.11 k1.13 k1.15 k1.1 k1.5 k1.7 k1.3 u1.5 to u1.15). Theory G (POOL issues at 0.55 us each and in an order that is not the order of readiness: k1.15:9 is issued 3.5 us after its evacuation and holds u1.8's buffer, u1.5:9 and u1.7:9 stand behind later ones): k1.4's wait (1.18 to 1.28) falls to 0.6, u1.8 waits under 0.3, the last u shuffle is issued by 43.6, i1's end comes 0.8 to 1.5 earlier: 175.5 to 176.2 (178.4 and 176.9 for the two kernels it is made from). Rival F (DMA engines full, landings as late): 176.8 to 178.4.

The median is 175.44 against 176.94, and 3.0 us less than with the tables early alone. Its PE timeline over the same stretch:

```profile
36.75 0.62 PE L1126 MATMUL ps<-arena 128*128 128x128 f16 x8
...
41.27 8.39 PE L1112 MATMUL ps<-arena 128*64 128x448 bf16 x68 [0.18 <-DVE arena L761]
```

The waits of 0.87 and 0.89 at 37 and 43 are gone; 0.18 is left. i1 ends at 71.52, 1.3 earlier than after the change, and earlier than in any of the profiles of the same lists named above, though ScalarE waits longer for k and ssm_k at the start than in the kernel after (1.15 against 0.69 us, here on ScalarE):

```profile
10.05 1.93 ACT L757 COPY arena<-ps 128x1024 bf16<-128x1024 bf16 x2 [1.15 <-PE ps L1056]
```

### Repairs together, and what is left

"Tables early", "one shuffle earlier" and "TZ early" in one kernel; then "shuffles when ready" with "TZ early", that is with the new front and the old order of the rest; then this with two kT copies back on VectorE and u1.1, u1.2 on ScalarE, which is about 1.0 us less work for the two engines; then with the old ending of i1; then with both of these.

```diff
 "act", both repairs and kT back
-kv.7:8 kT.5:8 kT.1:8 u1.0:8 tables.6:3
+kv.7:8 tables.6:3 u1.0:8 u1.1:8 u1.2:8
...
 "dve", both repairs and the old ending of i1
-xn.0:1 i1.15:0 q.4:3 i1.16:0
+xn.0:1 i1.16:0 i1.15:0 q.4:3
```

> The kernel of the run before with the early tables and with u1.1:10 right behind u1.3:9 on POOL. Theory E: POOL is free for the shuffles, k1.4's and k2.6's waits both fall under 0.3, i1 ends 1.0 to 2.0 earlier than in the run before: 171.3 to 172.4. Rival F: no earlier landings, 173.0 to 173.5.

> The same order of shuffles and tables in the mixture of the new front with the old MLP and early TZ transfers (173.86). Theory G: 172.3 to 173.0, no PE wait over 0.3 us between 36 and 44. Rival F: 173.6 to 174.2.

> The run before with two kT copies (kT.1, kT.5) back on VectorE and u1.1 and u1.2 on ScalarE in exchange, tables.6:2 ahead of kv.9's products and its Sin right behind kv.7: about 1.0 us of evacuation time less in the front. If the work that the change added counts in full: 0.3 to 0.6 less than the run before. If PE (without a gap from 13 to 36 us) sets the pace there: within 0.2 of it.

> The mixture with early tables and shuffles by readiness (172.23) with the end of i1 as before the change: i1.16:0 ahead of i1.15:0 on VectorE, i1.16:18 ahead of i1.16:9 on ScalarE with xn.1 behind both, and the matmuls and transfers in the same order. In that kernel i1 ended at 71.79 and mlp.0 began 7.8 us behind it, before the change 7.3. Theory H (xn.1 in front of the last two evacuations costs 0.4, and the pair of transfers that POOL issues last 0.4): 0.5 to 0.8 less, 171.4 to 171.8. Rival: the distance is set by the layernorm's own chain from i2.3 to Q[0], 172.0 to 172.4.

> The kernel of the run before with kT.1 and kT.5 on VectorE and u1.1 and u1.2 on ScalarE. If the evacuation work that the change added counts in full: i1's end 0.3 to 0.6 earlier than in the run before, and the median by as much lower, 170.9 to 171.4. If PE and the loads set the pace up to 36 us: within 0.2 of the run before.

In that order the ratios are 1.0105 [1.0069, 1.0140], 1.0108 [1.0072, 1.0145], 1.0143 [1.0098, 1.0187], 1.0101 [1.0059, 1.0144] and 1.0147 [1.0107, 1.0186]. The windows of the second, "both repairs", over ScalarE's front and the MLP:

```profile
5.09:71.79 66.70, 62.36 (x887) 32.39 (x884) 63.72 (x100) 61.93 (x73) 35.26 (x86) 1.00 0.78 265
...
79.61:167.66 88.05, 87.98 (x477) 56.12 (x476) 26.55 (x60) 22.15 (x48) 14.35 (x37) 1.00 0.44 171
```

The two repairs, of which the second brings the old order of the rest with it, take 4.7 of the 6.5 us back (172.23). The MLP is whole, PE busy 87.98 of 88.05. What remains in the profile is i1's end, +0.85, 79.61 - 71.79 = 7.82 up to the first MLP matmul, +0.5, and the MLP, +0.1: together 1.4 of the 1.8 us by which the medians differ. The other 0.4 lies outside the profiled span, and no run here shows where it comes from.

Less work on ScalarE and VectorE gained nothing, twice: by the ratios the two kernels are 0.6 and 0.8 us slower than without it, which neither of the two expectations gave. The profiles do not say why. The third kernel ends i1 at 71.25, 0.54 earlier than the second, but its w1a.1 is released 5.97 us behind that instead of 4.62, and mlp.0 comes 10.32 behind instead of 7.82; the last ends i1 at 72.57, 0.49 later than the kernel with the old ending alone (72.08). Both are within what two profiles of the same front differ by, so whether i1's end follows the evacuation work plus the waits, on which the forecast's sum rests, is not settled by these two. That PE sets the pace up to 36 us fits the windows shown above, but no run took work off PE there. The old ending of i1 did nothing either, where 0.5 to 0.8 us was expected of it, and the TZ transfers landed 5.53 us behind i1's end with it: what sets that landing is not the order of i1's last evacuations, and stays open. The first kernel of this group shows that the order by readiness is one way and not the only one: tables early and one shuffle earlier, each worth nothing or less alone, reach the same ratio together on top of "TZ early" (which alone had 1.0185). None of them is faster than the kernel before.

## Why the prediction was wrong, step by step

**What bounds the kernel.** The second machine was read rightly: its 87.94 us come back nearly whole with the old order of the rest (88.69), and with "TZ early" too (88.05). The first left PE out. Up to 36 us PE was busy 30.05 of 31.29 us before, so the two great holes of ScalarE (2.33 and 1.02) faced a PE that had 1.24 us to spare in all that time; by these rows little more than a microsecond could be won there by order alone, which is an estimate that no run tests. That "no order makes that shorter; it can start earlier or be interrupted" was the sentence to take seriously: it was interrupted.

**(a) Evacuations.** Right in sign and nearly in size. ScalarE's work up to i1's end is 61.75 against 59.57, +2.18, where +1.8 stood; VectorE's is 63.68 against 64.16, -0.5, where 0.0 to -0.3 stood.

**(b) Sin first.** Right: Sin at 5.09 (near 5.2 forecast), -0.65 where -0.5 stood.

**(c) Loads and waits of the front. This step failed.** The two old holes went as forecast, v0 and the kv products came in time (10.60 to 12.82; 12.5 forecast). But ScalarE stood 67.73 - 61.75 = 5.98 us idle, where 65.20 - 59.57 = 5.63 stood before: waits went up by 0.35 where -2.1 were forecast. With +2.18 and -0.65 this is the +1.88. Up to 36 us they fell, from 5.14 to 4.11 us, by half of what was forecast; behind 36 they rose, from 0.49 to 1.87. The hand count began at 19 us and ended at 38, and inside it two waits are left, 1.18 at k1.4 and 0.38, together 1.56 against the 1.25 that stood: k1.4 waited 1.18 where 0.6 was counted, because u1.1's second shuffle was issued only at about 24.1. More was left out on both sides. Ahead of 20, ScalarE waited 2.34 us in six pieces among the kT copies (the three greatest are in its timeline above). The ssm_k parts, pushed to places 7 to 11 of SP's queue, are issued from 4.0 to 6.0 us (1.6 to 3.3 before) and land 4.8 to 8.9 us after that (5.3 to 8.4), and their landing was never followed; but PE stood only 1.20 us for them, and the rest of the 2.34 is PE's own queue, which the count did not follow either. Behind 36, PE waited 0.87 and 0.89 for the first stage's last shuffles and buffers, because the order of the shuffles on POOL is not the order in which they are ready; "shuffles when ready", which also has the tables early, removes both and gains 1.5 us. The price of the late ssm_k itself is shown only from one side: moving it ahead of v0 costs more than it saves. VectorE's check failed with it: its last product ends at 70.35 and not at 68.1, with 4.44 us of waits instead of 2.62.

**(d) From i1 to the MLP.** Failed: +0.74 where -0.23 stood. Q[0] is not what mlp.0 waits for: VectorE started it at 79.68, and mlp.0 came 1.20 later (77.68 and 0.58 before). From the landing of the last TZ transfers to mlp.0 kernels with the new i2 order take 3.54 to 4.03 us (3.54 after), with the old order 2.98 to 3.36 (3.06 before). Two kernels lie outside: "old PE rows and banks" takes 5.93 with its wait for a bank, and "both repairs and kT back" 4.35, in which eight i2 matmuls take 2.42 us, where ten take 2.30 in the kernel after. The difference is about +0.5, of i2 matmuls that now stand ahead of mlp.0 on PE. i2.58 was booked as a gain, but PE runs without a gap from 77.37 to mlp.0, so its two matmuls filled no hole: they add 0.38 us here. The other 0.26 is the landing itself, 4.52 us behind i1's end instead of 4.26.

**(e) The MLP on PE. This is the step that cost most.** The place was nearly named (idle between 84 and 95; the waits for Q run from 91.15 to 96.50), the cause was not. W1 was priced with a slack of 0.4 to 1.0 us, at +0.1. The other sentence of that step, that Q[8] to Q[15] are wanted earlier and VectorE has "under 1 us to spare", got no price, and it decided: +2.64. The view of waits of the kernel after says it in two lines (who waits, for whom, us in all, times, the longest):

```profile
PE ps L1459 <- DVE arena L1412: 1.8, 3, 1.0
...
DVE arena L1412 <- POOL arena L1405: 4.9, 6, 1.2
```

It is not VectorE's queue that is tight but POOL's chain of tiny operations: Q[6] begins 91.10 - 80.88 = 10.2 us behind the first MLP matmul and Q[10] at 95.93, and shuffled rows ask for them sooner. The supply is later too: before the change Q[6] began 9.16 us behind the first MLP matmul. Sorting the rows takes 1.2 us of it back; the old order of i2, gates and MLP leaves 88.69 - 87.94 = 0.75 of it, and 0.11 with "TZ early". How the rest divides between banks, gates and the i2 order, which also makes Q later, is not settled.

**(f) Tail.** Right: +0.24 (+0.25).

**The rivals.** (1) Late u shuffles: the last issue was at 45.3, not 42.2, and they were late, but VectorE reached the first product only at 49.58, so the wait is not at i1.0: the same cause showed earlier, in (c), at the buffers. (2) W1 late: 0.45 us where Q does not hide it, nothing in the kernel after. (3) "The waits return" is the nearest to what the front did, but its price was bounded by the old waits. (4) did not occur. The range failed with them: each rival was priced alone, and (c), (d) and (e) went wrong together.
